# Issuing the first score matmuls twice, with a new instruction order, in a fused attention and MLP kernel

## The chip, the cores and the metric

The kernel runs on one core of one Trainium2 chip. The metric is the device time of one execution in microseconds (us), from the first to the last instruction. A core has five engines that each work through their own list of instructions in order: TensorE (PE, matmuls; its weight loads are listed as PEld), VectorE (DVE), ScalarE (ACT), GpSimd (POOL) and SyncE (SP, which here only issues transfers). Sixteen DMA engines move data.

## The reference, cut to what matters

Attention with root-mean-square normalised queries and keys (8 batches, 12 heads, 448 positions, head size 64), whose output is the input of a two-layer MLP with a hard-swish.

```python
def rmsnorm(x, g):
    rms = np.sqrt(np.mean(x * x, axis=-1, keepdims=True) + 1e-06)
    return x / rms * g
q_n, k_n = (rmsnorm(q, g_q), rmsnorm(k, g_k))
scores = scale * np.matmul(q_n, k_n.transpose(0, 1, 3, 2))
scores = scores - np.max(scores, axis=-1, keepdims=True)
attn = np.exp(scores)
attn = attn / (np.sum(attn, axis=-1, keepdims=True) + 1e-09)
attn_out = np.matmul(attn, v)
x = attn_out.transpose(0, 2, 1, 3).reshape(B * S, H * D)   # 3584 x 768
h = x @ w_in                                               # 768 x 2048
relu6 = np.clip(h + 3.0, 0.0, 6.0)
out = (h * relu6 / 6.0) @ w_out                            # 2048 x 768
```

## The kernel before

The body does not issue instructions at once. It adds operations to a plan, each with the engines that it may run on ("ways"), and at the end the plan issues them in the sequence of a long list, ORDER. A table WAY says for which operations another than the first engine is taken. An operation's number is its place in the sequence in which the body adds operations. Each engine then keeps to the sequence in which its instructions were issued.

```python
ORDER = [
    8, 10, 9, 11, 30, 38, 31, 12, 32, 13, 33, 34, 14, 66, 35, 15, 36, 64, 16, 37, 65, 17, 39, 68, 40, 18, 71,
    # ... 2,348 numbers in all
]

def add(self, ways, want, fn, reads=(), writes=(), load=(), since=0.0, soon=()):
    i = len(self.ops)
    self.way[i] = WAY.get(i, 0)
    eng, occ, fin = ways[self.way[i]]
    # ... predecessors from reads and writes

def emit(self, order):
    # ...
    for i in order:
        self.ops[i][4](self.ops[i][0])
```

A head pair P is two heads of one batch; there are 48, six to a batch. Pairs 0 to 5 are batch 0, pairs 6 to 11 batch 1. Queries, keys and values of two pairs come with one load each (`load`), into three buffers in turn. The last 64 of the 448 rows of each head come with loads of their own (`load_rest`, tiles `rr` and `vr`, operations called "rest" below).

```python
qk_r = ring(NQK, [TP, 2, 2, FULL], FP32, "qk")    # NQK = 3
eT_r = ring(NE, [TP, T, S2 + 2 * PAD], BF16, "eT")  # NE = 2
S_r = [psum.tile([128, 2, 512], FP32, name=f"S{i}") for i in range(2)]
M_r = [psum.tile([128, 512], FP32, name=f"M{i}") for i in range(2)]

def load(P, want, parts="kqv", n=1, first=False):
    # ...
    em((nc.scalar if e == ACT else nc.sync).dma_start(
        out=dst.rearrange("p o (h x) -> p (o h) x", h=2),
        in_=src[b, hs, 0:T * TP].rearrange("h (p t) d -> p h (t d)", t=T)))
```

`prep` squares them (L507 on GpSimd or L505 on ScalarE), sums the squares on VectorE (L517), takes the power -1/2 on ScalarE (L522, L525), and scales keys and queries into `qke` (even pairs) or `qko` (odd pairs) on GpSimd or VectorE (L542). `trans` transposes these on TensorE (L640) for pairs 0 to 12 and copies the result to `T`; later pairs are transposed by the DMA.

The weights of the MLP come in four blocks each, issued by GpSimd among its other work:

```python
def weights():
    for c in range(4):
        def f_i(_, c=c):
            cols = slice(c * 512, (c + 1) * 512)
            em(nc.gpsimd.dma_start(
                out=w_in_sb[:, :, cols], in_=moe_w_in[:, cols].rearrange("(k p) n -> p k n", p=128)))
        plan.add([(POOL, 0.8, 3.0)], -20.0, f_i, [], [("w_in", c)], load=(4.56, 95), since=AT_IN[c])
    # ... and w_out alike
```

The scores of a pair: for each of three key tiles t, two matmuls, one for each head, on different 64 rows of TensorE, and then one exponential on ScalarE (L687) for both. A further matmul (L697) takes the rest of the keys of both heads at once. `av` multiplies with the values (L722), `finish` divides by the row sums (L736, L739) and transposes (L756).

```python
def score(slots, want):
    parts = [(P, t, *((X_ps, ("X",)) if wide else sbank())) for P, t, wide in slots]

    def f_s(_):
        for P, t, ps, _ in parts:
            qkT = T_r[P // 2 % NT]
            q0, k0 = queries(P), (KO if P % 2 else KE) + t * TP
            for a in range(2 if P >= ND else 4):
                r = slice(a % 2 * 64, a % 2 * 64 + 64)
                em(nc.tensor.matmul(                                     # L677
                    out=ps[:, a % 2, 0:S], lhsT=qkT[r, k0:k0 + TP], rhs=qkT[r, q0:q0 + S],
                    start=True, stop=True))
    # ...
```

With ND = 0 each matmul is issued once. The hidden layer of the MLP, in groups f of 128 columns; each needs all six pairs of its batch and one of the two banks M:

```python
def h_group(b, f, want, dt, nb):
    ps, res = bank(nb)
    # ... six matmuls into ps, L776
    def f_r(eng):       # the limiter, on ScalarE (L787) or VectorE (L789)
        if eng == ACT:
            em(nc.scalar.activation(out=ts[:], in_=ps[:, 0:S], func=RELU, bias=3.0, scale=1.0))
        else:
            em(nc.vector.tensor_scalar(ts[:], ps[:, 0:S], -3.0, 3.0, A_MAX, A_MIN))
    def f_g(_):         # the gate, on VectorE (L793); after it the bank is free
        em(nc.vector.scalar_tensor_tensor(
            out=gT[:, f, e * S:(e + 1) * S], in0=ts[:], scalar=lim, in1=ps[:, 0:S], op0=op, op1=A_MULT))
```

`y_group` is the second layer (L813), whose results go out with SyncE. At the start the kernel issues matmuls on zeros (`warm`, L397), which compute nothing that is used.

Of the kernel before, what the change touches and what calls it, by code (L numbers as in the profile page):

```python
# [22 lines left out]
WAY = {65: 1, 66: 1, 77: 1, 81: 1, 82: 2, 83: 2, 84: 2, 86: 1, 88: 1, 90: 1, 92: 1, 99: 1, 101: 2, 103: 1,  # L23
    107: 1, 108: 1, 118: 1, 119: 2, 124: 1, 130: 1, 138: 1, 151: 1, 160: 1, 162: 2, 163: 1, 164: 2, 172: 1,
    197: 1, 201: 1, 203: 2, 225: 1, 226: 1, 234: 1, 236: 1, 261: 1, 262: 1, 273: 1, 275: 1, 288: 1, 289: 1,
    306: 1, 320: 1, 335: 1, 343: 1, 347: 1, 351: 1, 355: 1, 359: 1, 363: 1, 371: 1, 375: 1, 387: 1, 391: 1,
    397: 1, 408: 1, 418: 1, 446: 1, 455: 1, 456: 2, 458: 1, 463: 1, 489: 1, 490: 1, 496: 2, 526: 1, 527: 1,
    529: 1, 536: 1, 553: 1, 564: 1, 566: 1, 589: 1, 590: 2, 592: 1, 597: 1, 609: 1, 620: 1, 624: 1, 632: 1,
    636: 1, 640: 1, 650: 1, 655: 1, 663: 1, 667: 1, 671: 1, 675: 1, 679: 1, 683: 1, 688: 1, 712: 1, 713: 1,
    714: 1, 723: 1, 724: 1, 725: 2, 777: 1, 779: 1, 795: 1, 822: 1, 846: 2, 874: 1, 894: 1, 898: 1, 902: 1,  # L30
    917: 1, 925: 1, 940: 1, 952: 1, 956: 1, 967: 1, 971: 1, 976: 1, 977: 1, 983: 1, 988: 1, 1001: 1,
    1002: 1, 1011: 2, 1012: 1, 1013: 1, 1018: 1, 1048: 1, 1053: 1, 1066: 1, 1077: 2, 1078: 2, 1086: 1,
    1120: 1, 1121: 1, 1130: 1, 1131: 2, 1132: 2, 1133: 1, 1141: 1, 1155: 1, 1165: 1, 1174: 1, 1178: 1,
    1182: 1, 1186: 1, 1190: 1, 1205: 1, 1209: 1, 1213: 1, 1217: 1, 1231: 1, 1236: 1, 1240: 1, 1244: 1,
    1250: 1, 1256: 2, 1283: 1, 1284: 1, 1293: 1, 1312: 1, 1313: 1, 1319: 1, 1335: 1, 1336: 1, 1337: 1,
    1346: 2, 1348: 1, 1367: 1, 1368: 1, 1374: 1, 1382: 1, 1391: 1, 1401: 1, 1411: 1, 1421: 1, 1425: 1,
    1429: 1, 1440: 1, 1449: 1, 1453: 1, 1468: 1, 1480: 1, 1484: 1, 1490: 1, 1507: 1, 1522: 1, 1526: 1,
    1532: 1, 1538: 1, 1546: 1, 1564: 1, 1565: 1, 1575: 1, 1595: 1, 1609: 1, 1617: 1, 1627: 1, 1629: 1,
    1630: 2, 1638: 1, 1649: 1, 1682: 1, 1683: 1, 1684: 1, 1707: 1, 1711: 1, 1730: 1, 1734: 1, 1746: 1,
    1752: 1, 1757: 1, 1761: 1, 1769: 1, 1773: 1, 1777: 1, 1783: 1, 1788: 1, 1792: 1, 1796: 1, 1808: 2,  # L40
    1834: 1, 1835: 1, 1836: 1, 1837: 1, 1864: 1, 1871: 2, 1879: 1, 1887: 1, 1897: 1, 1899: 2, 1900: 2,
    1920: 1, 1934: 1, 1953: 1, 1954: 1, 1963: 1, 1977: 1, 1981: 1, 2001: 1, 2005: 1, 2024: 1, 2032: 1,
    2036: 1, 2042: 1, 2047: 1, 2051: 1, 2055: 1, 2059: 1, 2078: 1, 2106: 1, 2116: 1, 2117: 1, 2118: 1,
    2127: 1, 2135: 1, 2142: 1, 2165: 1, 2209: 1, 2228: 1, 2236: 1, 2255: 1, 2259: 1, 2263: 1, 2267: 1,
    2271: 1, 2275: 1, 2281: 1, 2290: 1, 2317: 1, 2328: 1, 2334: 1}


class Plan:
# [13 lines left out]
# [4 lines that stand above are left out]
# [34 lines left out]
    8, 10, 9, 11, 30, 38, 31, 12, 32, 13, 33, 34, 14, 66, 35, 15, 36, 64, 16, 37, 65, 17, 39, 68, 40, 18, 71,  # L100
    67, 69, 70, 19, 41, 74, 72, 42, 77, 91, 73, 43, 75, 20, 44, 76, 45, 92, 81, 46, 78, 21, 93, 47, 79, 85,
    96, 48, 94, 22, 49, 80, 86, 101, 50, 51, 95, 23, 52, 97, 82, 53, 98, 87, 100, 99, 24, 54, 106, 89, 55,
    123, 56, 25, 90, 57, 88, 108, 58, 26, 83, 102, 59, 84, 104, 103, 131, 124, 27, 105, 60, 132, 61, 28, 62,
    125, 63, 133, 29, 143, 134, 139, 121, 107, 188, 126, 144, 140, 141, 109, 120, 118, 122, 163, 145, 127,
    165, 142, 185, 119, 128, 152, 164, 146, 186, 110, 167, 129, 111, 147, 166, 193, 148, 113, 187, 168, 173,
    112, 190, 149, 153, 175, 117, 150, 174, 195, 116, 177, 178, 115, 258, 196, 179, 176, 151, 137, 191, 180,
    162, 138, 197, 181, 182, 171, 192, 114, 172, 154, 183, 130, 135, 1, 194, 136, 155, 226, 224, 184, 189,
    204, 203, 156, 169, 205, 206, 161, 160, 259, 158, 207, 170, 159, 481, 216, 198, 210, 0, 212, 484, 217,
    213, 211, 237, 214, 2, 215, 218, 261, 199, 238, 235, 219, 240, 262, 239, 220, 482, 221, 200, 157, 241,
    246, 263, 417, 222, 202, 208, 247, 201, 248, 418, 483, 244, 264, 223, 265, 249, 209, 250, 267, 251, 245,  # L110
    269, 415, 236, 266, 270, 242, 252, 416, 253, 243, 225, 271, 254, 276, 255, 301, 300, 3, 277, 227, 278,
    256, 4, 279, 268, 257, 302, 288, 228, 260, 229, 303, 280, 234, 281, 232, 486, 282, 283, 233, 304, 309,
    487, 284, 285, 230, 310, 274, 479, 311, 286, 231, 312, 287, 289, 419, 272, 313, 275, 314, 420, 6, 315,
    273, 316, 307, 317, 290, 457, 426, 318, 421, 478, 422, 427, 305, 308, 423, 319, 291, 485, 329, 330, 306,
    331, 424, 332, 320, 333, 321, 322, 292, 323, 293, 458, 324, 296, 428, 334, 325, 295, 326, 335, 437, 298,
    446, 336, 438, 327, 294, 752, 489, 341, 328, 445, 429, 342, 430, 297, 337, 343, 433, 344, 431, 434, 338,
    432, 549, 447, 349, 490, 339, 439, 5, 448, 435, 350, 436, 340, 459, 449, 450, 351, 460, 440, 453, 345,
    480, 352, 454, 425, 346, 441, 461, 491, 452, 462, 357, 451, 550, 463, 347, 358, 492, 299, 348, 493, 464,
    466, 495, 749, 465, 353, 467, 359, 494, 354, 360, 468, 456, 365, 469, 355, 366, 356, 497, 7, 367, 442,
    361, 498, 685, 368, 518, 362, 455, 553, 373, 499, 363, 374, 364, 500, 375, 443, 369, 501, 370, 376, 504,  # L120
    444, 502, 371, 747, 505, 516, 381, 503, 382, 372, 552, 506, 470, 383, 471, 686, 554, 517, 507, 472, 377,
    384, 473, 555, 530, 556, 528, 474, 557, 519, 531, 389, 551, 390, 558, 532, 475, 533, 378, 580, 520, 534,
    521, 535, 496, 476, 524, 379, 537, 525, 477, 536, 380, 538, 508, 539, 523, 391, 509, 510, 522, 540, 392,
    511, 385, 743, 688, 526, 579, 560, 512, 513, 561, 398, 386, 562, 563, 387, 514, 564, 565, 388, 566, 567,
    515, 393, 568, 687, 527, 569, 541, 542, 570, 543, 544, 593, 559, 545, 591, 546, 594, 394, 595, 395, 598,
    742, 600, 689, 599, 399, 581, 400, 690, 601, 547, 696, 750, 582, 691, 692, 693, 548, 713, 694, 583, 571,
    584, 572, 573, 697, 589, 587, 574, 588, 575, 698, 576, 701, 586, 729, 401, 712, 753, 702, 577, 703, 396,
    578, 585, 748, 704, 602, 714, 603, 397, 754, 744, 604, 402, 605, 715, 404, 596, 695, 724, 405, 606, 716,
    590, 488, 406, 717, 779, 719, 755, 407, 721, 403, 607, 409, 756, 811, 757, 408, 410, 722, 699, 777, 411,
    810, 608, 412, 720, 812, 609, 1034, 718, 610, 413, 730, 746, 705, 813, 611, 814, 815, 745, 614, 612, 414,  # L130
    816, 615, 613, 706, 707, 616, 618, 1035, 758, 597, 617, 619, 723, 807, 725, 759, 529, 726, 592, 620, 727,
    708, 621, 622, 1036, 709, 728, 623, 710, 731, 624, 735, 732, 736, 625, 733, 626, 808, 700, 734, 764, 627,
    778, 630, 628, 780, 761, 711, 762, 737, 631, 629, 760, 763, 738, 835, 766, 632, 975, 634, 834, 976, 739,
    751, 740, 767, 768, 635, 790, 973, 633, 781, 770, 836, 741, 771, 977, 636, 638, 782, 769, 637, 786, 639,
    978, 974, 791, 785, 809, 787, 792, 640, 772, 773, 794, 783, 642, 641, 979, 980, 765, 796, 788, 793, 643,
    784, 1030, 774, 797, 646, 775, 1040, 798, 837, 644, 789, 647, 776, 799, 800, 801, 645, 802, 1001, 1000,
    821, 803, 838, 818, 839, 804, 841, 846, 819, 651, 842, 805, 817, 652, 820, 851, 1041, 648, 1002, 847, 825,
    844, 806, 1003, 823, 826, 1042, 649, 824, 827, 840, 1032, 1043, 828, 1004, 653, 1033, 795, 982, 650, 829,
    1005, 1044, 830, 1045, 848, 981, 1038, 831, 849, 654, 845, 1031, 843, 657, 850, 655, 1094, 853, 832, 1065,
# [90 lines left out]
def kernel(  # L230
# [129 lines left out]
    LW = 0.6  # L360
    RW = 0.34
    MG = 2
    NW0 = 8
    NW1 = 22
    W1 = 0.35
    ND = 0


    plan = Plan()
    MM_FIN = 0.17  # L370

    def act(n, more=0.0):
# [621 lines left out]
```

## Time and profile before

| | before |
|---|---|
| time, median of two runs | 442.01 us (441.74 to 442.29) |
| span of the profiled execution | 441.2 us |
| TensorE busy | 417.0 us (95%) |
| VectorE busy | 271.2 us (61%) |
| ScalarE busy | 251.9 us (57%) |
| GpSimd busy | 175.1 us (40%) |
| mean granted TensorE clock | 0.981 of full speed |
| moved by DMA | 64.21 MB, mean 146 GB/s |
| hidden layer (L776) on TensorE | 714 matmuls recorded, 156.4 us busy |
| second layer (L813) on TensorE | 752 matmuls recorded, 137.6 us busy |
| scores (L677) on TensorE | 234 matmuls recorded, 36.2 us busy |

How to read the lines that follow below. The page of a profile shows each engine's busy share in forty equal slices of the span as a row of digits (9 is 90% or more); PEclk is the clock that TensorE was granted, in tenths. A table of stretches gives for each engine its busy time and its number of instructions. A line of the timeline gives start and duration in us, engine, source line, operation, and what it writes and reads; in brackets stands how long the engine was idle before, and what ended that. The chain of waits is the chain of work that ended last, followed back from the end. Busy matmuls overlap one another, so that TensorE's busy time is not its work at peak speed.

### The profile page before, as it was taken

How to read it: one execution, taken by the hardware profiler on the slowest of the kernel's cores; microseconds unless marked ns; L12 is line 12 of the kernel's file. 1: busy time of each engine (PE TensorE's matmuls, PEld its weight loads, DVE VectorE, ACT ScalarE, POOL GpSimd, SP SyncE). 2: the span in 40 equal slices, each digit the busy share in tenths (PEclk: the TensorE clock that was granted, in tenths of full speed). 3: DMA queues.
4: the chain of work that ended last, by engine and by line, in shares of the span. 5: the costliest groups of instructions: out<-in, count | busy, mean ns of one | idle time of the engine just before them, and what ended most of it. 6: DMA issues, size and time to landing. Idle time of an engine off the chain costs nothing.

```text
span 441.2 us, 9375 instructions
## 1 busy us (share of the span) xinstructions
PE 417.0 (95%) x3629; PEld 242.4 (55%) x3629; DVE 271.2 (61%) x519; ACT 251.9 (57%) x490; POOL 175.1 (40%) x286
## 2 busy tenths in 40 slices
PE   7687769999999999999999999999999999999997
PEld 7344434565554655565555565565655555655554
DVE  6566639967968777766767748745555455334331
ACT  4877645886888767574776545665564433321011
POOL 5598436567585555535544545304400000000000
PEclk9968969999999999999999999999999999999999
DMA  6699999819998999467688566635343121020103
GB/s 199 192 231 210 225 248 255 232 31 219 169 238 214 223 210 280 119 185 188 105 192 192 128 126 174 129 80 111 77 85 78 30 57 53 37 83 1 71 22 122
DMA packets 121392, 64.21 MB, mean 146 GB/s; under 512 B 75524, under 2 KB 117892, under 8 KB 121348
## 3 DMA queue, kind: packets, MB, share of 16 engines
q1 hardware_dynamic: 115664, 57.17, 55.0%
q0 software_dynamic: 5248, 6.29, 8.1%
q8 instruction: 28, 0.46, 0.4%
q10 hardware_dynamic: 436, 0.16, 0.1%
q14 instruction: 16, 0.13, 0.1%
HBM read 45.61 MB, written 11.01 MB: 128 GB/s over the span
## 4 chain that ended last, share of the span: by engine, by line
PE 81%; DMA 9%; DVE 4%; POOL 2%; ACT 2%; issue 1%; SPq 1%; ACTq 0%; DVEq 0%; POOLq 0%
PE M L813 28%; PE M L776 28%; PE X L722 9%; PE S L677 5%; DMA qk<-in_q_dram 5%; PE S L813 4%; DMA vr<-in_v_dram 2%; PE S L697 2%; DMA qk<-in_k_dram 2%; PE X L776 1%; PE X L677 1%; PE S L776 1%; DVE gT L793 1%; PE X L813 1%; DVE ts L789 1%
## 5 line engine op out<-in xcount | busy, mean ns | idle before, releaser
L776 PE MATMUL M<-xT,w_in_sb 128*128 128x448 bf16 x714 | 156.4, 355 | 1.7 <-DVE gT L793 0.8
L813 PE MATMUL M<-w_out_sb,gT 128*128 128x384 bf16 x752 | 137.6, 326 | 0.0
L687 ACT ACTIVATE eT<-S 128x896 bf16<-128x896 f32 x117 | 104.6, 915 | 43.9 <-PE S L677 43.3
L813 PEld LDWEIGHTS <-gT 128*128 128x128 bf16 x912 | 85.3, 98 | 59.3 <-issue 7.3
L776 PEld LDWEIGHTS <-w_in_sb 128*128 128x128 bf16 x768 | 71.6, 98 | 66.4 <-issue 11.6
L793 DVE SCALAR_TENSOR_TENSOR gT<-ts,M 128x448 bf16<-128x448 f32 x119 | 73.6, 619 | 31.1 <-ACT ts L787 28.5
L789 DVE TENSOR_SCALAR ts<-M 128x448 f32<-128x448 f32 x77 | 47.9, 622 | 39.4 <-PE M L776 38.5
L507 POOL TENSOR_TENSOR sq<-qk 128x384 f32<-128x384 f32 x59 | 48.2, 830 | 45.7 <-DMA qk<-in_q_dram 21.5
L517 DVE TENSOR_REDUCE ssq<-sq 128x12 f32<-128x768 f32 (+4 forms) x51 | 51.2, 1023 | 13.2 <-POOL sq L507 11.1
L722 PEld LDWEIGHTS <-eT 128*128 128x128 bf16 x1152 | 46.5, 99 | 17.3 <-issue 3.6
L722 PE MATMUL X<-va,eT 128*128 128x65 bf16 x1152 | 49.9, 195 | 1.9 <-ACT eT L687 1.2
L542 POOL TENSOR_TENSOR qko<-qk,rs 128x384 bf16<-128x384 f32 x46 | 37.1, 827 | 26.4 <-DMA T<-qko 21.0
L787 ACT ACTIVATE ts<-M 128x448 f32<-128x448 f32 x42 | 22.7, 544 | 35.7 <-PE M L776 35.3
L677 PE MATMUL S<-T 64*128 64x448 bf16 x234 | 36.2, 365 | 3.3 <-ACT eT L687 1.8
L542 POOL TENSOR_TENSOR qke<-qk,rs 128x384 bf16<-128x384 f32 x46 | 37.8, 826 | 2.9 <-DMA T<-qke 1.7
L739 DVE TENSOR_TENSOR xn<-X,rd 128x512 bf16<-128x512 f32 x48 | 33.1, 690 | 1.4
L823 ACT ACTIVATE y<-M 128x384 f32<-128x384 f32 x25 | 12.3, 493 | 35.3 <-PE M L813 35.0
L701 ACT ACTIVATE eR<-S 128x448 bf16<-128x448 f32 x48 | 26.3, 549 | 4.5 <-PE S L697 4.4
L505 ACT ACTIVATE sq<-qk 128x384 f32<-128x384 f32 x37 | 18.7, 520 | 15.5 <-DMA qk<-in_k_dram 10.6
L826 DVE TENSOR_SCALAR y<-M 128x384 f32<-128x384 f32 x22 | 12.2, 555 | 24.3 <-PE M L813 24.2
L677 PEld LDWEIGHTS <-T 64*128 64x128 bf16 x288 | 11.0, 94 | 25.9 <-issue 17.8
L687 ACT ACTIVATE eT<-X 128x896 bf16<-128x896 f32 x27 | 24.7, 916 | 0.0
(84 smaller groups left out, 342.8 us busy)
## 6 DMA issues: line engine op xcount, KB each, us to landing
vf<-in_v_dram SPq DMA_DIRECT2D x24, 384.0 KB, 4.7
qk<-in_k_dram SPq DMA_DIRECT2D x23, 384.0 KB, 5.1
qk<-in_q_dram SPq DMA_DIRECT2D x23, 384.0 KB, 4.9
out_dram<-y SPq DMA_DIRECT2D x23, 384.0 KB, 3.3
w_in_sb<-in_moe_w_in_dram POOLq DMA_DIRECT2D x4, 768.0 KB, 12.2
w_out_sb<-in_moe_w_out_dram POOLq DMA_DIRECT2D x4, 768.0 KB, 13.3
out_dram<-y SPq DMA_DIRECT2D x9, 192.0 KB, 3.2
rr<-in_q_dram SPq DMA_DIRECT2D x28, 48.0 KB, 3.8
```

The lines of the kernel that those rows point to most:

```text
L507: em(nc.gpsimd.tensor_tensor(out=o, in0=src, in1=src, op=A_MULT))
L517: em(nc.vector.tensor_reduce(out=ssq[:, c0:c1], in_=sq[:, c0 * D:c1 * D].rearrange("p (n d) -> p n d", d=D), axis=AX_X, op=A_ADD))
L542: em((nc.vector if e == DVE else nc.gpsimd).tensor_tensor(out=qks[:, b0:b0 + T].rearrange("p t h d -> p h t d"), in0=src, in1=rs[:, c0:c0 ...
L677: em(nc.tensor.matmul(out=ps[:, a % 2, 0:S], lhsT=qkT[r, k0:k0 + TP], rhs=qkT[r, q0:q0 + S], start=True, stop=True))
L687: em(nc.scalar.activation(out=eT[:, t, PAD:PAD + S2].rearrange("p (a s) -> p a s", a=2), in_=ps[:, :, 0:S], func=EXP, bias=0.0, scale=1.0))
L701: em(nc.scalar.activation(out=eR_r[P % NE][:, PAD:PAD + S], in_=ps[:, 0, 0:S], func=EXP, bias=0.0, scale=1.0))
L722: em(nc.tensor.matmul(out=X_ps[:, i // 2, o:o + (E1 if t < T else 2 * E1)], lhsT=eT[:, t, c0:c0 + TP] if t < T else eR[:, c0:c0 + TP], rhs ...
L739: em(nc.vector.tensor_tensor(out=xn[:].rearrange("p (a i) h d -> p a (i h) d", a=2), in0=xv[:, :, :, 0:D], in1=rd[:].unsqueeze(3).to_broad ...
L776: em(nc.tensor.matmul(out=ps[:, 0:S], lhsT=w_in_sb[:, kt, f * 128:(f + 1) * 128], rhs=xT[:, kt, x0:x0 + S], start=(kt == 0), stop=(kt == N ...
L789: em(nc.vector.tensor_scalar(ts[:], ps[:, 0:S], -3.0, 3.0, A_MAX, A_MIN))
L793: em(nc.vector.scalar_tensor_tensor(out=gT[:, f, e * S:(e + 1) * S], in0=ts[:], scalar=lim, in1=ps[:, 0:S], op0=op, op1=A_MULT))
L813: em(nc.tensor.matmul(out=ps[:, 0:nc0], lhsT=gT[:, f, i * 128:(i + 1) * 128], rhs=w_out_sb[:, f, c0:c0 + nc0], start=(f == 0), stop=(f == ...
```

## The change

The change sets ND from 0 to 6. For head pairs 0 to 5 (batch 0), each score matmul is issued twice, with the same operands into the same place, so that the result is the same. The second issue computes nothing new. It is meant to keep TensorE active in the opening part, where it waits much, so that it is granted its full clock. With this, ORDER and WAY have been sought anew for the whole kernel, so that the sequence on every engine differs from early on, also where nothing is added: the loads and weight blocks, the engine on which a square or a limiter runs, and the matmuls of later batches. Nothing else differs.

```diff
@@ -363,7 +361,7 @@
     NW0 = 8
     NW1 = 22
     W1 = 0.35
-    ND = 0
+    ND = 6
@@ -20,29 +20,27 @@ (the table of engines, cut)
-WAY = {65: 1, 66: 1, 77: 1, 81: 1, 82: 2, 83: 2, 84: 2, 86: 1, 88: 1, 90: 1, 92: 1, 99: 1, 101: 2, 103: 1,
+WAY = {64: 1, 66: 1, 67: 1, 80: 1, 82: 2, 83: 2, 90: 1, 91: 1, 103: 1, 118: 1, 119: 2, 130: 1, 138: 1,
 ...
@@ -97,132 +95,132 @@ (the order, cut)
-    8, 10, 9, 11, 30, 38, 31, 12, 32, 13, 33, 34, 14, 66, 35, 15, 36, 64, 16, 37, 65, 17, 39, 68, 40, 18, 71,
+    8, 10, 9, 11, 30, 66, 38, 31, 12, 32, 13, 33, 34, 14, 35, 15, 36, 64, 16, 37, 68, 65, 17, 39, 69, 40, 18,
 ...
```

The order on two engines, with the numbers resolved to what they do, up to where the two versions matter for the loads. GpSimd, from its squares of pairs 4 and 5 on (before, then after):

```
before: square k4, square q5, rest k2, va 3, w_in 1, square q6, rest q4, rest k4 x2, w_in 0, vb, w_in 2,
        square k7, square q7, scale k4, scale q5, square k9, scale q7, scale k7, square rest 6, vb x2,
        w_in 3, w_out 0, square k8, rest k6, scale q6, scale k6, rest k6, square rest 8, w_out 2, vb,
        scale k9, scale q9, rest k8 x2, rest q8, scale k8, square k10, scale q8, square q10, w_out 1, ...
after:  square q5, square k4, w_in 0, va 4, square k5, square q6, rest k4, square q7, square k7, va 6,
        rest k4, scale q4, w_in 3, scale q7, scale k7, square k9, w_in 1, w_in 2, w_out 0, square rest 8,
        scale q6, scale k6, rest k6 x2, w_out 1, square k8, vb, scale k9, square rest 10, scale q9,
        scale q8, scale k8, rest k8 x2, vb, square q11, square q10, ...
```

ScalarE and VectorE around the first hidden-layer groups:

```
before, ACT: square rest 10, limiter f0, square k11, exp, square q11, limiter f2, ...
after,  ACT: exp x2, square k11, square k10, limiter f1, limiter f0, exp x2, limiter f3, ...
before, DVE: limiter f1, gate f1, gate f0, copy T, limiter f3, gate f3, copy T, sum 10, gate f2, ...
after,  DVE: copy T, gate f1, copy T, gate f0, sum 11, sum 10, gate f3, gate f2, ...
```

## Prediction

> **What bounds the kernel now.** First the page's forty slices, to see where the time is not TensorE's; a slice is 11.03 us.
>
> ```profile
> PE   7687769999999999999999999999999999999997
> PEclk9968969999999999999999999999999999999999
> DMA  6699999819998999467688566635343121020103
> ```
>
> From the seventh slice (66 us) on, TensorE is at 9 and at full clock; before it, it is at 6 to 8, with a clock of 0.6 to 0.8 in the third, fourth and sixth slice, while the DMA engines are at 9 from the third slice to the seventh. So there are two stages, and I looked at each by itself. In the late one, the waits of TensorE from 70 us on come to 1.6 us in all (0.8 is the longest), and the chain that ended last has 354 us of TensorE in the 371 us from 70 to 441. A gain there can only be pieces of the other 17 us. The early stage I cut into stretches (length, then busy us of PE, PEld, DVE, ACT, POOL, granted clock, DMA share, GB/s):
>
> ```profile
> 26.00:34.00 8.00, 7.74 (x58) 3.86 (x58) 5.17 (x12) 6.84 (x13) 7.15 (x11) 0.50 1.21 206
> ...
> 47.00:54.00 7.00, 5.72 (x48) 2.95 (x44) 4.76 (x7) 3.90 (x9) 3.44 (x6) 1.00 1.17 223
> 54.00:59.00 5.00, 0.08 (x1) 0.08 (x2) 0.00 (x0) 1.33 (x2) 1.61 (x2) 0.73 1.14 229
> 59.00:63.00 4.00, 4.00 (x21) 2.12 (x22) 0.42 (x1) 0.75 (x2) 0.70 (x1) 0.50 1.15 262
> ```
>
> Two things stand out: 8 us at half clock with TensorE full, and a hole at 54 to 59 us in which no engine works while the DMA runs flat out. The timeline says who ends the hole:
>
> ```profile
> 57.14 0.52 ACT L505 ACTIVATE sq<-qk 128x384 f32<-128x384 f32 x1 [6.14 <-DMA qk<-in_k_dram]
> 57.26 0.82 POOL L507 TENSOR_TENSOR sq<-qk 128x384 f32<-128x384 f32 x1 [6.23 <-DMA qk<-in_k_dram]
> 58.04 0.83 POOL L542 TENSOR_TENSOR qke<-qk,rs 128x384 bf16<-128x384 f32 x1
> 58.92 0.61 PE L640 MATMUL S<-identity,qke 128*128 128x128 bf16 x4 [5.87 <-POOL qke L542]
> ...
> 62.30 0.83 POOL L507 TENSOR_TENSOR sq<-qk 128x384 f32<-128x384 f32 x1 [3.43 <-DMA qk<-in_q_dram]
> 63.16 1.22 DVE L517 TENSOR_REDUCE ssq<-sq 128x16 f32<-128x1024 f32 x1 [3.16 <-POOL sq L507]
> 64.29 0.61 DVE L793 SCALAR_TENSOR_TENSOR gT<-ts,M 128x448 bf16<-128x448 f32 x1
> ```
>
> Following ORDER by counting the operations as the body adds them gives these lines their names. The squares at 57.26 and 62.30 are of head pair 10 (those on ScalarE of pair 11), not needed by TensorE yet. But engines work in order: the key square stands ahead of the scaling of pair 8's queries (58.04), and TensorE has that pair's transposes ahead of ready hidden-layer matmuls; the reduction at 63.16 stands ahead of the gate of hidden group f=2 (64.29). So k and q of pairs 10 and 11 hold everything. Why they are late is in the chain of waits and the issues:
>
> ```profile
> 40.60 21.63 DMA qk<-in_q_dram
> 62.30 0.84 POOL sq L507
> ```
> ```profile
> 24.93 1.01 POOL L850 DMA_DIRECT2D w_in_sb<-in_moe_w_in_dram  x1
> 28.51 0.88 POOL L850 DMA_DIRECT2D w_in_sb<-in_moe_w_in_dram  x1
> 30.15 0.82 POOL L850 DMA_DIRECT2D w_in_sb<-in_moe_w_in_dram  x1 [0.16 <-issue]
> 39.38 0.88 POOL L850 DMA_DIRECT2D w_in_sb<-in_moe_w_in_dram  x1
> 40.26 0.76 POOL L855 DMA_DIRECT2D w_out_sb<-in_moe_w_out_dram  x1
> ```
>
> The q load takes 21.6 us where the fastest qk load takes 2.5: weight blocks share the DMA engines with it (a sixth goes out at 44.91). In the stretch from 38.5 to 41 us the weights' queue has 78.8% of the engines' time and SyncE's 39.0% (they overlap). The 393 kB of q landed 5.1 us after k, so SyncE's queue then moves 77 GB/s; from 24 to 32 us, with fewer weight blocks waiting, it moved 1.17 MB, 146 GB/s.
>
> **What the Trainium skill says.** "DMA: Bandwidth & Descriptors", section "Queues, rings and completion order": each DMA engine serves in turn the queues that have work, a packet at a time. That agrees with the two shares above. "TensorE: Matmul & The Clock Gate", section "Part 1: The HAM clock gate": the clock is halved after an idle window of about 3.4 us and comes back after a busy one. The trace agrees: 0.50 in 59 to 63, right after the hole. The same page, section "Part 3: Packing small matmuls": matmuls in different row groups run together. The trace agrees: a score pair (two 64-row matmuls of 448) takes 0.36 us, the one 128-row score of the rest 0.35, and two pairs in a row 0.55, so a further pair costs 0.19.
>
> **The change, part by part.**
>
> *Doubled scores.* Six head pairs x three key tiles x two matmuls are 36 more, in 18 pairs at 0.19: 3.4 us of TensorE at full clock, at most 9.5 at half clock, where a second pair costs 1.09 - 0.56 = 0.53. All lie between 14 and 46 us, where TensorE is busy 24.6 of 32 us and ScalarE's 24 exponentials of 0.91 us or loads set the pace. Each lengthens one score-to-exponential step by 0.19 us, mostly behind the exponential of the other score bank. What it is for: more activity near 18 to 26 us, so that the clock of the 26 to 34 us stretch isn't halved. 7.7 busy us there would be some 4 at full clock; ScalarE's 6.84 us then bounds the stretch, so at most 1 us comes off. And the loads behind it don't come sooner for that. I book 0 to -1 us.
>
> *New order of loads and weights.* SyncE's queue holds the same 34 rows up to the q load in question, 7.8 MB in both. GpSimd's list differs. Before: w_in blocks 1, 0, 2 close together, then w_in 3 and w_out 0. After: w_in 0 behind the squares of pairs 4 and 5, as now, at about 25; then va (0.50), two squares (1.65), a rest (0.39), two squares (1.61), va (0.50), a rest (0.39), a scaling (0.83) = 5.9 us; then w_in 3 at about 32; two scalings and a square (2.4); then w_in 1, w_in 2, w_out 0 in a row from about 35. So between 25 and 32 us one weight block competes in place of three, and SyncE's queue runs ahead nearer 146 than 77 GB/s. From 32 on it is slowed again. Ahead of and with q there are then roughly two 393 kB loads, four small ones (0.2 MB), k and q: 1.77 MB, 23 us at 77 GB/s, which would be 55; with a part of it gone earlier, 50 to 58. I take 54 as an estimate, against 62.2.
>
> *New order on the in-order engines.* The false block goes: on GpSimd both of pair 8's scalings now stand ahead of the squares of pairs 10 and 11. Another comes: ScalarE now has the two key squares ahead of its first hidden-layer relu (f=1), and VectorE the two reductions ahead of the gate of f=3, one group earlier than now. So the hole does not go; it ends when q lands. From 54: square 0.83, first reduction 0.95, then the second 1.22 (behind the second square at 55.7) = 57.1; gates f=3 and f=2, 1.3 = 58.4; reciprocal and scaling 0.9; relu and gate of f=5, 1.25 = 60.6. Then group f=7 may start on TensorE. Before it starts at 66.26. That is 5.7 us sooner.
>
> *A second check.* The next loads (pairs 12, 13) landed at 57.4 + 8.5 = 65.9 (q) and 59.2 + 8.3 = 67.5 (k), by issue and time to landing. The DMA work ahead of them is the same, so I leave them near 65; in the new list their square stands ahead of the relu of f=6, on which f=8 waits: f=8 at about 66.5, against 71.44. That is 4.9 us sooner, and pair 7's values (0.95 us in the chain for 28 matmuls) and a group of transposes (0.22) now stand ahead of f=8 instead of behind it: 6.1 us. The two checks agree.
>
> *The rest.* From f=7 on, the TensorE work left is the same but for two groups of transposes (0.4 us) that now stand ahead of it; it runs at full clock, and takes 375 us to the end now. The new order moves hidden-layer relus from VectorE to ScalarE (VectorE was busy 9.57 of 10 us at 70 to 80), which may help; the late order I can't price: 0, give or take 2 us.
>
> Sum: 442.0 - 5.7 - 0.5 (clock) + 0 = 435.8. Every step that I found gives something back only if none of the new in-order neighbours blocks. I know of one (a value row of batch 1 is now issued after 30 us and stands on VectorE ahead of pair 5's division), and put 0.9 us on it: 436.7.
>
> **Rivals.** (1) The loads are bound by total DMA work, so q lands near 62 again. For it: 1.1 and more of DMA share without a break from 24 to 80 us; against: queue order decides which bytes come first. Then f=7 starts at 69, the doubled scores buy nothing: 443 to 445. (2) TensorE's added 3.4 us fall on the path, with the half clock still there. For it: 7.74 of 8 us busy at 26 to 34. Against: the loads end that stretch. Alone it makes 443 to 445; on top of my gain, 439. (3) The hole closes wholly and the clock stays full from 14 us on: for it, nothing but loads keeps ready matmuls waiting; this gives 8 to 10 us, 432 to 434. Against: the reductions still stand ahead of the gates.
>
> **Range and chances.** Landing of q between 50 and 58 is worth +-4 us, the late order +-2, a new block up to +3. So 436.7, from 431.5 to 443.5. Two per cent is 8.8 us: below 433.2 needs rival 3 (0.20); above 450.9 needs rival 1 and a loss in the late stage (0.04); within, 0.76.
>
> **What would show it.** Right: q of pairs 10 and 11 landing at 50 to 58; TensorE idle in one hole shorter than 5 us; f=7 at 59 to 63; a clock over 0.8 at 26 to 34; 370 to 376 us from f=7 to the end; 72 more score rows (matmuls and weight loads). Wrong: q at 62, a hole elsewhere before 70 us, the half clock still at 26 to 34, or late waits of over 4 us on VectorE.

## Result and profile after

| | before | after |
|---|---|---|
| time, median of two runs | 442.01 us (441.74 to 442.29) | 435.78 us (435.51 to 436.06) |
| ratio, with 95% interval | | 0.9859 (0.9817 to 0.9901) |
| span of the profiled execution | 441.2 us | 434.3 us |
| mean granted TensorE clock | 0.981 | 0.992 |
| first matmul of hidden group f=7 | 66.26 us | 60.49 us |
| from there to the end | 374.9 us | 373.8 us |

The change takes 6.2 us, 1.4%, off. Of the 6.9 us between the two spans, 5.8 lie ahead of f=7 and 1.1 behind it. The first matmuls of f=7, before and then after:

```profile
66.26 1.30 PE L776 MATMUL M<-xT,w_in_sb 128*128 128x448 bf16 x6
```
```profile
60.49 0.73 PE L774 MATMUL M<-xT,w_in_sb 128*128 128x448 bf16 x3
```

The page of the profile after, in the three rows that were read before:

```profile
PE   5977899999999999999999999999999999999996
PEclk8799999999999999999999999999999999999999
DMA  7899999969799996975796736552433211010014
```

TensorE now stays at 9 from the sixth slice (54 us) on instead of the seventh, and its clock is at 9 from the third slice on. But the first slice fell from 7 to 5: something was lost at the start. The stretches of the early stage, with the columns of before (length, busy us of PE, PEld, DVE, ACT, POOL, granted clock, DMA share, GB/s):

```profile
26.00:34.00 8.00, 5.72 (x68) 3.04 (x69) 6.55 (x14) 5.81 (x13) 8.00 (x12) 1.00 0.94 191
...
47.00:54.00 7.00, 6.22 (x83) 4.26 (x84) 4.80 (x14) 6.28 (x15) 5.67 (x11) 1.00 1.18 231
54.00:59.00 5.00, 5.00 (x38) 2.37 (x38) 4.54 (x8) 4.13 (x9) 2.84 (x4) 1.00 1.17 232
59.00:63.00 4.00, 4.00 (x30) 2.09 (x29) 2.71 (x6) 3.70 (x9) 3.08 (x7) 1.00 1.16 206
```

The hole at 54 to 59 is gone: TensorE is busy for all of it, where it had 0.08 us. The half clock at 26 to 34 is gone too. Now the loads, in the timeline of after: the weight blocks, and k and q of head pairs 10 and 11.

```profile
28.98 1.01 POOL L848 DMA_DIRECT2D w_in_sb<-in_moe_w_in_dram  x1
35.61 0.37 SPq L431 DMA_DIRECT2D qk<-in_k_dram  x1
36.66 0.88 POOL L848 DMA_DIRECT2D w_in_sb<-in_moe_w_in_dram  x1
36.74 0.37 SPq L431 DMA_DIRECT2D qk<-in_q_dram  x1
39.91 1.71 POOL L848 DMA_DIRECT2D w_in_sb<-in_moe_w_in_dram  x2
```

And the DMA view of after, cut to the moment of each of the two issues; the last number is the time to landing:

```profile
qk<-in_k_dram SPq DMA_DIRECT2D x1, 384.0 KB, 5.2
qk<-in_q_dram SPq DMA_DIRECT2D x1, 384.0 KB, 5.3
```

So k landed at 40.8 and q at 42.0, where q had landed at 62.2; the q load takes 5.3 us and not 21.6. No engine waits for them any more. The chain of waits says the same for the whole: its share of DMA fell from 9% to 3%, and TensorE's rose from 81% to 85%. What was lost at the start stands in the two timelines. Before:

```profile
2.17 0.87 ACTq L403 DMA_DIRECT2D gr_t<-in_g_q_dram  x1
3.07 0.22 ACTq L403 DMA_DIRECT2D gr_t<-in_g_k_dram  x1
...
5.06 0.38 PE L413 MATMUL X<-ones_t,g_t 1*128 1x1 f32 x2 [0.45 <-DVE g_t L408]
```

After:

```profile
4.56 0.31 ACT L503 ACTIVATE sq<-rr 128x128 f32<-128x128 f32 x1 [1.12 <-DMA rr<-in_q_dram]
4.59 0.50 ACTq L401 DMA_DIRECT2D gr_t<-in_g_q_dram  x1
5.13 0.22 ACTq L401 DMA_DIRECT2D gr_t<-in_g_k_dram  x1
...
8.37 0.28 DVE L406 SCALAR_TENSOR_TENSOR g_t<-gr_t 1x128 f32<-1x128 f32 x1 [1.87 <-DMA gr_t<-in_g_k_dram]
8.71 0.58 PE L411 MATMUL X<-ones_t,g_t 1*128 1x1 f32 x2 [4.10 <-DVE g_t L406]
```

The new order puts ScalarE's first square, which waits for its own load until 4.56, ahead of the issue of the two small loads of the gain vectors. TensorE then waits 4.10 us for the gains, where it waited 0.45. Its first attention-value matmul comes at 19.35 instead of 15.52.

### The profile page after: what moved, and what is told of

Its sections match the earlier page's. It is cut to its first block, busy times and chain, and to the rows that moved or that the text cites. A ratio compares the mean times of both kernels' runs of the same rounds, so it can differ in the third digit from the quotient of the medians.

```text
span 434.3 us, 9488 instructions
## 1 busy us (share of the span) xinstructions
PE 415.9 (96%) x3665; PEld 243.2 (56%) x3665; DVE 264.5 (61%) x519; ACT 259.4 (60%) x509; POOL 170.4 (39%) x277
## 4 chain that ended last, share of the span: by engine, by line
PE 85%; DVE 4%; ACT 3%; DMA 3%; POOL 2%; issue 1%; ACTq 0%; SPq 0%; DVEq 0%; POOLq 0%
PE M L774 29%; PE M L811 28%; PE X L720 9%; PE S L675 5%; PE S L811 4%; ACT eT L685 2%; PE S L695 2%; DMA rr<-in_q_dram 2%; PE X L774 1%; PE X L395 1%; PE X L675 1%; PE S L774 1%; POOL sq L505 1%; DVE gT L791 1%; PE X L811 1%
## 5 line engine op out<-in xcount | busy, mean ns | idle before, releaser
L685 ACT ACTIVATE eT<-S 128x896 bf16<-128x896 f32 x117 | 103.5, 915 | 31.6 <-PE S L675 31.5
L785 ACT ACTIVATE ts<-M 128x448 f32<-128x448 f32 x68 | 37.1, 546 | 53.9 <-PE M L774 52.3
L505 POOL TENSOR_TENSOR sq<-qk 128x384 f32<-128x384 f32 x55 | 45.2, 833 | 39.8 <-DMA qk<-in_q_dram 23.2
L720 PEld LDWEIGHTS <-eT 128*128 128x128 bf16 x1152 | 45.3, 97 | 16.4 <-issue 5.2
L787 DVE TENSOR_SCALAR ts<-M 128x448 f32<-128x448 f32 x51 | 31.7, 622 | 22.1 <-PE M L774 21.7
L675 PE MATMUL S<-T 64*128 64x448 bf16 x270 | 38.2, 354 | 2.9 <-ACT eT L685 2.7
L821 ACT ACTIVATE y<-M 128x384 f32<-128x384 f32 x24 | 11.7, 497 | 40.9 <-PE M L811 40.8
L675 PEld LDWEIGHTS <-T 64*128 64x128 bf16 x324 | 12.0, 94 | 25.1 <-issue 19.5
L390 POOL CAST va<-vf 128x384 bf16<-128x384 f32 x20 | 10.4, 525 | 37.4 <-PE X L720 29.8
```

Of the source, the lines that this page charges most:

```text
L505: em(nc.gpsimd.tensor_tensor(out=o, in0=src, in1=src, op=A_MULT))
L675: em(nc.tensor.matmul(out=ps[:, a % 2, 0:S], lhsT=qkT[r, k0:k0 + TP], rhs=qkT[r, q0:q0 + S], start=True, stop=True))
L685: em(nc.scalar.activation(out=eT[:, t, PAD:PAD + S2].rearrange("p (a s) -> p a s", a=2), in_=ps[:, :, 0:S], func=EXP, bias=0.0, scale=1.0))
L720: em(nc.tensor.matmul(out=X_ps[:, i // 2, o:o + (E1 if t < T else 2 * E1)], lhsT=eT[:, t, c0:c0 + TP] if t < T else eR[:, c0:c0 + TP], rhs ...
```

## Experiments

Times are medians. A difference between two kernels is meant only where their intervals allow it; the kernel before, run beside them, gave 441.96, 441.45 and 441.77 us in the three groups below. Wherever a diff names w_in or w_out, the blocks' issues on GpSimd are moved and nothing else.

### What are the doubled scores worth?

Four pairs of kernels bear on it, two of them further below. First the two that separate it from the order: the changed kernel with single scores, and the kernel before with doubled ones.

```diff
 # the changed kernel
-    ND = 6
+    ND = 0
```

> The changed kernel with ND = 0: each score once, the new order kept. Theory A (order of loads): the gain is that of the weight blocks and loads; the doubled scores are worth nothing: 434.8 to 436.8 us, f=7 of the hidden layer starts at 60 to 62 us, even if the clock drops for a few us before 45. Theory B (clock): the doubled scores keep TensorE at full clock between 14 and 46 us, and that is the gain: half clock for 5 us and more in that stretch, 438.5 to 442 us. If the added matmuls cost time on the path: 432 to 434.5.

Measured: 436.65 us, ratio to before 0.9882 (0.9842 to 0.9922), f=7 at 61.20 us, and a granted clock of 1.00 at 14 to 34 us without any doubling. So the order alone keeps 5.3 us of gain, against 6.3 for the changed kernel run again below (435.15); the intervals of the two overlap, so that a part of about 1 us for the doubled scores is neither shown nor excluded.

```diff
 # the kernel before
-    ND = 0
+    ND = 6
```

> The kernel before with ND = 6 alone, old order. Theory A: the hole at 54 to 59 us stays, ended by k and q of pairs 10 and 11 at 57 and 62 us: 441 to 444 us, whatever the clock does at 26 to 34 us. Theory B: the clock at 26 to 34 us rises from 0.50 to over 0.9, and the time falls to 436 to 439 us.

Measured: 442.11 us, ratio 0.9998 (0.9974 to 1.0022). The stretches of this kernel, in the columns used above:

```profile
26.00:34.00 8.00, 7.05 (x56) 2.98 (x57) 4.13 (x11) 5.21 (x10) 6.83 (x11) 0.57 1.07 192
...
54.00:59.00 5.00, 2.47 (x13) 1.11 (x12) 1.80 (x4) 1.33 (x2) 1.61 (x2) 0.81 1.14 229
```

With the doubled scores the clock is still 0.57 at 26 to 34, and about half of the hole is still there (TensorE waits 2.53 us in one piece, where it waited 5.87). In the old order the added matmuls cost nothing and brought nothing that the times show; the new order has the gain, or all but a small part of it.

### Is it the later weight blocks?

One part of the new order alone, in the kernel before: w_in 0 takes the place of w_in 1, which goes behind pair 9's and 7's work on GpSimd, and w_in 2 goes next to w_in 3.

```diff
 # the kernel before, GpSimd's order
-  ..., va 3, w_in 1, square q6, rest q4, rest k4 x2, w_in 0, vb, w_in 2, square k7, ...
-  ..., scale q7, scale k7, square rest 6, vb x2, w_in 3, w_out 0, square k8, ...
+  ..., va 3, w_in 0, square q6, rest q4, rest k4 x2, vb, square k7, ...
+  ..., scale q7, scale k7, w_in 1, square rest 6, vb x2, w_in 2, w_in 3, w_out 0, square k8, ...
```

> The kernel before with the four blocks of w_in issued later by GpSimd: block 0 at 25 us, block 1 behind the scalings of pair 7 (about 36 us), blocks 2 and 3 at about 39 us; nothing else moved, scores once. Theory A: k and q of pairs 10 and 11 land 8 us or more earlier (under 54 us), the hole at 54 to 59 us closes, and the time is 435 to 439 us. Theory B, or a theory in which the squares' place in the order makes the hole: 441 to 443 us.

Measured: 434.92 us (434.11 to 435.84), ratio 0.984 (0.9793 to 0.9886): the whole gain of the change. The blocks went out at 25.77, 37.89 and 40.07 (two), k and q at 36.41 and 37.12, and k landed in 4.8 us. Two stretches of this kernel:

```profile
26.00:34.00 8.00, 7.18 (x57) 3.70 (x55) 4.99 (x11) 5.72 (x12) 5.58 (x10) 0.50 0.98 179
...
54.00:59.00 5.00, 5.00 (x41) 2.57 (x40) 4.84 (x8) 3.38 (x7) 2.91 (x6) 1.00 1.19 217
```

The hole is closed while the clock at 26 to 34 us is halved as before, and f=7 starts at 59.84, no later than in the changed kernel. So the gain does not need the full clock there, one of the two things that stood out in the profile before.

How the loads get faster is in the DMA view of 34 to 42 us, queue by queue (packets, MB, share of the 16 engines): first the kernel before, then this one. q0 carries GpSimd's weight blocks, q1 the loads of the other engines.

```profile
q0 software_dynamic: 1154, 1.16, 85.1%
q1 hardware_dynamic: 1151, 0.54, 34.6%
```
```profile
q1 hardware_dynamic: 3864, 2.20, 102.2%
q0 software_dynamic: 51, 0.05, 3.8%
```

In the kernel before the two queues move the same number of packets, 1154 and 1151, but one of weights holds 1.16 MB / 1154 = 1005 bytes and one of loads 0.54 MB / 1151 = 469. The loads so get a third of the bytes: 0.54 MB in 8 us, 68 GB/s, and not half. With no weights beside them they get 2.20 MB, 275 GB/s. This is what the Trainium skill, "DMA: Bandwidth & Descriptors", section "Queues, rings and completion order", says (the engine takes turns between queues packet by packet); the equal counts agree with it.

The same with doubled scores on top, since they might be of use once the loads are out of the way:

```diff
 # the kernel with late weight blocks
-    ND = 0
+    ND = 6
```

> The kernel before with w_in issued late as in the run that moved only that, and each score of pairs 0 to 5 twice as well. There, with the loads out of the way, TensorE was granted half clock in 26 to 34 us and 0.76 in 34 to 47 us. Theory B in its second form (the clock pays once no load holds the stretch): clock over 0.9 from 14 to 47 us, and 431 to 433.5 us. Theory A alone (ScalarE, GpSimd and loads set the pace there at any clock): 434 to 436 us.

Measured: 435.4 us (434.09 to 438.56), ratio 0.987 (0.9827 to 0.9912). The clock at 26 to 34 is 0.81 and f=7 starts at 58.04, 1.8 us sooner than at half clock, but the time is not lower.

### The other way round, and two half measures

If late blocks are the cause, early ones should undo the change. In the changed kernel, w_in 1 and 2 go back to a few operations behind w_in 0, and w_in 3 to right ahead of w_out 0:

```diff
 # the changed kernel, GpSimd's order
-  ..., w_in 0, va 4, square k5, square q6, rest k4, square q7, ..., w_in 3, scale q7, scale k7, square k9,
-  w_in 1, w_in 2, w_out 0, ...
+  ..., w_in 0, va 4, square k5, square q6, w_in 1, rest k4, square q7, w_in 2, ..., scale q7, scale k7,
+  square k9, w_in 3, w_out 0, ...
```

> The changed kernel (scores twice) with the blocks of w_in issued earlier by GpSimd: block 1 three operations behind block 0, block 2 two behind that, block 3 ahead of w_out 0, so three blocks within 8 us as in the kernel before. Theory A (weight blocks issued early take the DMA engines from k and q of pairs 10 and 11): these land at 52 us or later, a hole of 2 us and more comes back before 65 us, and the time is 438 to 443 us. If the rest of the new order carries the gain: 435 to 437 us.

Measured: 437.39 us (436.85 to 438.09), ratio 0.9901 (0.9863 to 0.9939). That gives back about 2 us of 6, less than the theory asked: all four runs lie above all six of the changed kernel beside them (434.73 to 435.6), but 4 us of the gain stay. So late blocks are enough for the gain, but they are not the only way to it. The DMA view at 34 to 42 us of this kernel:

```profile
q0 software_dynamic: 1174, 1.17, 86.2%
q1 hardware_dynamic: 1171, 0.50, 33.8%
...
qk<-in_k_dram SPq DMA_DIRECT2D x1, 384.0 KB, 13.5
qk<-in_q_dram SPq DMA_DIRECT2D x1, 384.0 KB, 15.0
```

The queues are in the state of the kernel before, and the loads are slow again. But q was issued at 36.77, 3.8 us sooner than in the kernel before, and so landed at 51.8, soon enough: TensorE is busy 4.88 of the 5 us from 54 to 59. A likely cause of the sooner issue is that the first weight block still goes out 2.6 us later (27.57 against 24.93): from 24 to 34 us the queue of loads moved 1.90 MB here and 1.25 in the kernel before. A load may be slow, then, if it is early enough.

So I split the weight blocks in the kernel before into the three early ones and the two that went out right ahead of q. First the two late ones, moved from 39.38 and 40.26 to 45.66 and 46.53:

```diff
 # the kernel before, GpSimd's order
-  ..., vb x2, w_in 3, w_out 0, square k8, rest k6, scale q6, scale k6, rest k6, square rest 8, ...
+  ..., vb x2, square k8, rest k6, scale q6, scale k6, rest k6, w_in 3, w_out 0, square rest 8, ...
```

> The kernel before with only w_in 3 and w_out 0 moved, from just ahead of the issue of q (pairs 10 and 11) to some 4 us after it; w_in 1, 0 and 2 stay. Theory A (what delays q are the blocks queued beside it when it is issued): q takes 5 to 9 us and lands at 46 to 50, the hole of 54 to 59 closes, 435 to 437. Theory B (what delays it is the backlog of the three earlier blocks): k and q still issued at 39 to 41 and q lands at 55 or later, part of the hole stays, 439 to 442.

Measured: 438.94 us, ratio 0.9929 (0.9903 to 0.9955), with runs from 434.35 to 441.33. The traced execution (span 435.9) is one of the shorter ones: k and q are issued at 41.27 and 42.49, as late as theory B said, but k lands in 8.8 us and the hole is closed (5.00 us busy at 54 to 59, f=7 at 59.46), as theory A said; the square of q, at 54.55, waits for no load. The median has under half of the gain and lies in neither theory's range. Then the three early ones, moved to 27.92, 30.88 and 32.56:

```diff
 # the kernel before, GpSimd's order
-  ..., va 3, w_in 1, square q6, rest q4, rest k4 x2, w_in 0, vb, w_in 2, square k7, square q7, scale k4, ...
+  ..., va 3, square q6, rest q4, rest k4 x2, w_in 1, vb, square k7, square q7, w_in 0, scale k4, w_in 2, ...
```

> The kernel before with w_in 1, 0 and 2 each moved some 3 us later, to about where the changed kernel with early blocks had them (27.6, 30.6, 33.0); w_in 3 and w_out 0 stay. Theory A (the blocks beside q at its issue): q is still issued next to w_in 3 and w_out 0 and takes 15 us or more; it lands after 55 and the time stays at 440 to 442. Theory B (the earlier backlog): k and q are issued at 37 to 38, ahead of w_in 3, q lands at 52 or before, and the time is 435 to 438.

Measured: 441.21 us, ratio 0.9985 (0.9966 to 1.0004). Neither theory fits. Three blocks 3 us later let q go out 6.1 us sooner, at 34.48; its square starts at 52.84, about as early as theory B needs, and f=7 starts at 56.80; and still there is no gain. The timeline of this kernel shows why:

```profile
66.47 0.36 PE L677 MATMUL S<-T 64*128 64x448 bf16 x2
...
69.44 0.52 ACT L505 ACTIVATE sq<-qk 128x384 f32<-128x384 f32 x1 [6.01 <-DMA qk<-in_q_dram]
...
69.87 1.71 ACT L687 ACTIVATE eT<-S 128x896 bf16<-128x896 f32 x2
70.82 0.58 PE L640 MATMUL S<-identity,qke 128*128 128x128 bf16 x4 [3.99 <-ACT eT L687]
```

The hole has moved to the next loads. q and k of the next head pairs (12 and 13), issued at 48.09 and 51.03, take 21.3 and 23.7 us. ScalarE has the square of that q ahead of an exponential, and TensorE has transposes that wait for the exponential ahead of hidden-layer matmuls. It is the same block as in the kernel before, a pair later. The kernel with the late blocks alone escapes it: there q and k of 12 and 13 go out at 44.79 and 45.58 and take 9.3 and 12.5 us, though four blocks were issued in the 7 us ahead of them. What differs is SyncE's own queue: from 34 to 45 us it moved 2.36 MB there and 0.76 MB here, and here the values of pairs 10 and 11, issued at 36.69, land only at 57.2, so that q and k of 12 and 13 stand behind them.

### Is it the place of the squares in the order?

The rival to the loads: a load may be late if nothing that TensorE needs stands behind its square. In the kernel before, the squares and the sum of pairs 10 and 11 go behind the scaling, the exponentials, the limiter and the gate that they stood ahead of.

```diff
 # the kernel before
-  POOL: ..., scale k8, square k10, scale q8, square q10, w_out 1, ...
-  ACT:  ..., square k11, exp, square q11, limiter f2, exp (rest), ...
-  DVE:  ..., sum 10, gate f2, ...
+  POOL: ..., scale k8, scale q8, square k10, square q10, w_out 1, ...
+  ACT:  ..., exp, square k11, limiter f2, exp (rest), square q11, ...
+  DVE:  ..., gate f2, sum 10, ...
```

> The kernel before with four operations moved behind their neighbours on in-order engines: the key square of pair 10 behind the query scaling of pair 8 on GpSimd, the two squares of pair 11 behind exponentials of pair 6 on ScalarE, the sum of pair 10 behind the gate of f=2 on VectorE. Weights and scores as before. Theory A: the loads still land at 57 and 62 us, but fewer instructions stand behind them: half of the gain at most, 438 to 441 us. Theory E (the hole is made by the place of the squares, not by the loads): the hole at 54 to 59 us closes, 434 to 437 us.

Measured: 441.62 us, ratio 1.0001 (0.9978 to 1.0023), without even the part of the gain that theory A left open. The traced execution is one of the longest (444.49 us in runs from 438.41 to 444.73). The chain of waits of this kernel, "issue" steps of under 0.1 us left out:

```profile
41.80 21.07 DMA qk<-in_q_dram
...
62.94 0.84 POOL sq L507
...
63.80 1.23 DVE ssq L517
...
65.06 0.23 ACT rs L522
...
65.52 0.81 ACT eT L687
...
66.38 0.48 PE S L640 x3
```

The load is as slow as before, and now it blocks one step further down: the power of pair 10 (L522) still stands ahead of an exponential on ScalarE. The moves on three engines bring nothing while this neighbour stays. With the loads early, the same moves:

```diff
 # the kernel with late weight blocks: the moves of the last diff
```

> The kernel before with the w_in blocks late, and the squares and the sum of pairs 10 and 11 moved behind the work that TensorE waits for. Theory 1 (once k and q land at 42, their place on the in-order engines costs nothing): 434.5 to 435.5, the same as with the late blocks alone (434.92). Theory 2 (the in-order place still costs, behind the loads): 431 to 433.

Measured: 435.71 us (434.4 to 437.16), against 434.92 with the late blocks alone. Once the loads are early, the place of the squares costs nothing that can be seen.

### What did the change lose at the start?

The changed kernel with the two gain-vector loads ahead of ScalarE's first square:

```diff
 # the changed kernel, ORDER
-    8, 10, 9, 11, 30, 66, 38, 31, 12, 32, 13, ...
+    8, 10, 9, 11, 30, 38, 66, 31, 12, 32, 13, ...
```

> The changed kernel with one operation moved in the order: the loads of the two gain vectors are issued by ScalarE before its first square, as in the kernel before, not behind it. In the changed kernel the gains landed at 8.3 us instead of 4.7, and the first transposes ran at 12.05 us instead of 7.62. Theory C (the start is now on the path, since no load holds f=7 any more): 2 to 4 us less, 432 to 434 us. Theory D (the stretch to 60 us is bound by loads or by the amount of work on ScalarE and GpSimd): 435 to 436.5 us.

Measured: 434.23 us (433.08 to 435.66), ratio 0.9832 (0.9787 to 0.9876). Its traced execution (span 431.3 us) is the shortest of its four runs, and f=7 starts at 57.24. That is 3.3 us sooner than in the trace of the changed kernel above, and 2.2 sooner than in a second trace of the same kernel (59.47). The second waits for the gains nearly as long as the first (3.87 us), but TensorE has full clock at 12 to 14 us, where the first has half. So the loss at the start is real in the traces, at 2 to 3 us. The medians are read against the changed kernel run again unchanged:

> The changed kernel unchanged, beside the others on one chip: 435 to 436.5 us, in every theory. It gives the interval against which the single-score run and the gains-first run are read.

Measured: 435.15 us (434.73 to 435.6), ratio 0.9849 (0.9819 to 0.988). The intervals of the two overlap; a gain of 0.9 us from the early start is not shown. The last run asks whether the doubled scores help that early start:

```diff
 # the changed kernel with the gain loads first
-    ND = 6
+    ND = 0
```

> The changed kernel with the gain-vector loads moved ahead of the first square, and with single scores. Theory 1 (the doubled scores buy nothing anywhere, the lost start was the gain loads'): 434 to 435, within 1 us of the run with doubled scores and gain loads first (434.23). Theory 2 (with the early start the doubled scores keep the clock up and are worth their 3.4 us of TensorE): 436 to 438, and a granted clock under 0.7 somewhere in 14 to 47.

Measured: 436.98 us, ratio 0.9889 (0.9861 to 0.9917), with runs from 432.94 to 439.27, and a granted clock of 0.50 at 26 to 34 us, where the trace with doubled scores has 1.00. Both are what theory 2 said. The intervals against 434.23 just overlap, so that a worth of the doubled scores with the early start, 2.75 us by the medians, is not shown and not excluded. The traced execution (span 437.5) is the longest of the twenty. It starts f=7 at 56.63, sooner than any other kernel here. Then, in its timeline:

```profile
65.22 0.52 ACT L503 ACTIVATE sq<-qk 128x384 f32<-128x384 f32 x1 [5.71 <-DMA qk<-in_k_dram]
65.65 0.96 ACT L785 ACTIVATE ts<-M 128x448 f32<-128x448 f32 x2
66.21 1.15 DVE L791 SCALAR_TENSOR_TENSOR gT<-ts,M 128x448 bf16<-128x448 f32 x2 [6.85 <-ACT ts L785]
66.88 0.53 PE L774 MATMUL M<-xT,w_in_sb 128*128 128x448 bf16 x1 [4.54 <-DVE gT L791]
```

This is again the load of the next pair: k of pairs 12 and 13, issued at 44.72 behind the weights, lands after 20.5 us; its square stands ahead of the limiter, the limiter ahead of the gate, and TensorE waits 4.54 us for a bank. What was won in the first hole is given back in the second. Whether the half clock has a part in it stays open. SyncE is late already at its two `rr` loads from 36.25 us on, whose issue takes 5.44 us (2.52 in the trace with doubled scores, where k goes out at 41.34).

No kernel tried is shown to be faster than the changed one; the gain loads first (434.23) and the late blocks alone (434.92) beat the kernel before by as much, and the second does it with one part of the change.

## Why the prediction was right, and where its steps were not

436.7 us stood against 435.78, with the range holding it. The mechanism was the right one, but two of its steps missed and cancelled.

**What bounds the kernel: right.** k and q of pairs 10 and 11, slow beside the weight blocks, held the early stage; moving the blocks alone brings the whole gain. The half clock, named beside it as a second thing that stands out, was rightly given no more than 1 us: 434.92 with 0.50 at 26 to 34 us, 435.4 with 0.81.

**Doubled scores, 0 to -1 us: right in the old order, open in the new.** The added rows are there (270 matmuls recorded for 234, 324 weight loads for 288). In the old order, with loads early or late, they brought nothing that can be told from zero (442.11 for 441.96; 435.4 for 434.92). In the new order, taking them out cost 0.9 or 1.5 us (436.65 for 435.78 and 435.15) and, with the gains first, 2.75; all lie on the side of a gain, and none is clear of the intervals. The clock over 0.8 at 26 to 34 came, but not from the doubling alone: the single-scored changed kernel has it too, the kernel before with doubled scores has not, and with the gains first only the doubled one has.

**New order of loads and weights: right in direction, mis-sized.** "I take 54 as an estimate" for the landing of q; it landed at 42.0. The sum took 77 GB/s for SyncE's queue from 32 us on, as if weights were always waiting. At 34 to 42 us it moved 1.38 MB, 173 GB/s:

```profile
q1 hardware_dynamic: 2411, 1.38, 66.9%
q0 software_dynamic: 629, 0.63, 48.3%
```

GpSimd reached its blocks some 4 us later than I read from its list (28.98 for 25, 36.66 for 32, 39.91 for 35), since the whole start was late (with the gains first they go out at 25.72, 33.40 and 36.65), and q went out ahead of the last two w_in blocks instead of among them.

**"So the hole does not go; it ends when q lands": wrong.** The hole closed wholly, which was rival 3. I had set the sums ahead of the gates against it. They do stand there, and the timeline of after shows them at nearly the time that I gave them, but not because of q:

```profile
51.84 0.94 ACT L503 ACTIVATE sq<-qk 128x384 f32<-128x384 f32 x2
53.63 1.61 POOL L505 TENSOR_TENSOR sq<-qk 128x384 f32<-128x384 f32 x2
54.77 2.07 DVE L515 TENSOR_REDUCE ssq<-sq 128x12 f32<-128x768 f32 x2
56.76 0.61 DVE L791 SCALAR_TENSOR_TENSOR gT<-ts,M 128x448 bf16<-128x448 f32 x1
57.79 0.62 DVE L791 SCALAR_TENSOR_TENSOR gT<-ts,M 128x448 bf16<-128x448 f32 x1 [0.42 <-ACT ts L785]
```

q has been there for over 11 us when GpSimd gets to its squares, behind other work. The sums end at 56.8 (57.1 predicted) and the two gates at 58.4 (58.4 predicted), and TensorE, busy throughout 54 to 63, waits for none of it. So f=7 at 60.49 for 60.6 is right by two errors: the hole that I left in is not there, and all work comes later than I read, by a loss that I had not looked for, the gain vectors asked for behind a square. With them first, f=7 starts at 57.24, 9.0 us ahead of 66.26; the late start took 3.3 of these in this trace and 2.2 in the second. That the two errors came out equal was luck.

**The second check: right by the same accident.** Loads of pairs 12 and 13 were left "near 65"; k was issued at 44.60 and landed after 12.0 us, at 56.6. f=8 started at 66.03 for 66.5. That two checks agreed proved little, as both used a slow load queue and the same start.

**The late part: right.** 373.8 us from f=7 to the end, with 370 to 376 given; TensorE's waits from 70 us on are 1.1 us, where they were 1.6. The 0.9 us put on a new block by a value row are not seen as a wait of TensorE.

**What the rivals said.** Rival 1 (the total of DMA work sets the landing) fell: the loads take 5 or 21 us with all bytes moved alike. Rival 2 (the added matmuls on the path) fell with the unchanged time of the kernel before with doubled scores.

**Readings that were off without moving the sum much.** The load of 2.5 us has half the size (192 KB); loads of k of 384 KB have a median of 5.1. From 14 to 46 us there are 18 exponentials of 0.91 us, not 24. In the 5.1 us between the landings of k and q SyncE's queue moved 0.79 MB and not q's 0.39 alone, so the 77 GB/s are not read rightly, though near its rate at 34 to 45 us (0.70 MB, 64 GB/s). And the half clock at 26 to 34 us, unlike that at 59 to 63, is not explained by the idle window that the prediction cites: TensorE's longest wait from 17 us up to it is 0.91 us.

What stays open is the scatter: the kernels with only the two late blocks moved and with gains first and single scores spread over 7.0 and 6.3 us from run to run, the changed one run again over 0.9. The first two were run 20 times, the last six times, and the kernel before, with its hole, spread over 5.1 and 5.9 us in the first two groups. Only one execution of each of the two has a trace. That the hole of pairs 10 or 12 opens in some runs and not in others would explain it, but was not shown.

## What to carry to other kernels

A load on one queue and weights on another share the DMA engines packet for packet, so hold back what is needed last until the loads that an in-order engine will meet first have been issued; to shift it by 3 us may only move the hole to the next load. In a new order, look at what has changed in the first 10 us and behind which wait each small load is issued, not only at the stage that the change is for. A half clock or an idle slice need not be worth anything, as here in the old order: ask whether the next wait is for TensorE, and try it alone before paying for it.

## What was not expected

A load of 384 KB from SyncE took 4.8 us with hardly any weights moving beside it, 5.3 in the changed kernel, 15.0 with three blocks close ahead and 23.7 behind a backlog of its own queue as well; from one kernel to the next, moving three blocks by 3 us moved a landing by 9. The granted clock at 26 to 34 us did not follow the number of matmuls: 0.57 with doubled scores and 7.05 us of TensorE busy, 1.00 with single ones and 5.22 us busy in the changed order; and one kernel, the changed one, had 0.50 at 12 to 14 us in one execution and 1.00 in another. Half clock at 26 to 34 us, at 7.18 of 8 us busy, cost no time that shows at the end.
